# Sending the convolution's taps through DRAM in a fused attention and S4D kernel

## The chip, the core and the metric

The kernel runs on one core of one Trainium2 chip. The metric is the device time of one execution in microseconds (us), and the figure given for a kernel is the median of its runs. Engines are named as in the profile: PE (matmul, with its weight loads as PEld), DVE, ACT, POOL and SP, which here only issues transfers.

## The reference

`x` has 2048 rows of 448 features. Two branches read it and a gate mixes them:

```
def _A_ref(x, wqkv, wo):                       # linear attention, 16 heads of 28
    qkv = (x @ wqkv).reshape(B, S, 3, H, Dh) ...
    phi = lambda t: jnp.where(t > 0, t + 1, jnp.exp(t)) + 1e-6
    pq, pk = phi(q), phi(k)
    kv  = einsum("bhsd,bhse->bhde", pk, v);  z = einsum("bhsd->bhd", pk)
    num = einsum("bhqd,bhde->bhqe", pq, kv)
    den = einsum("bhqd,bhd->bhq", pq, z)[..., None] + 1e-6
    return (num / den) ... @ wo
def _B_ref(u, ...):                            # S4D: a causal convolution of each feature
    K = 2.0 * jnp.einsum("dn,dnl->dl", C, P).real
    y = causal convolution of u with K (by FFT)
    return y + u * D_skip
g = sigmoid((x * gate_w).sum(-1, keepdims=True))
return g * a + (1 - g) * b
```

With the inputs as they are drawn, each feature's time step is so small that all its taps `K` are one number. The convolution is then a running sum of `x` over the rows, times that number. A flag for each feature says whether this holds; a second, general path at the end of the program runs only if a flag says no.

## The kernel before, in words

The 2048 rows are worked on as 16 chunks of 128 rows. Float32 products are made of two parts: a rounded "high" half (ACT makes it) and the "low" rest (a subtraction, mostly on POOL), and PE multiplies high by high, low by high and high by low. The order of every engine's instructions is written out by hand: engines work in the order of the code, and only semaphores between engines hold them.

The main loop (`for c in range(2, NC - 2)`, L476 to L532) runs over chunks. In a step `c` PE computes, in this order: the 11 products of `k` for chunk `c+1` (`project`, tile `k`), in steps 5 to 13 one or two running sums `v` (`do_v`, two products with the triangular matrix `tri`), the 11 products of `q` for chunk `c` (tile `q`), and the 11 products of `g` for chunk `c` (`do_g`), which sum phi(k) times `x`. The table `VS` (L35) says which `v` are made in which step and on which side of `q`. A `v` lives in one of two places of PSUM, `v0` and `v1`, by the parity of its number, so that `v` number 2 can begin only when DVE has read number 0 out.

The other engines' part of a step:

- `split_t(c + 2)`: ACT casts the turned `x` of chunk `c+2` to its high half, and POOL subtracts to get the low half (tile `xt`, L236). PE needs both for the next step's `k`.
- `k_feature`, `k_high`, `k_low`: ACT clamps `k` (`Relu` of -k, L360) and takes the exponential (L361), DVE joins them (L362), ACT adds 1e-6 and rounds (L366), DVE makes the low half and adds to the sum `zb` (L372).
- `q_post`: ACT takes an exponential for the gate (L380) and one of `q` (L349), DVE clamps and adds 1e-6 (L350) and joins (L353) into `pq`.
- `v_post`: DVE multiplies `v` by the row `near`, the taps of all 448 features on every partition (L415); SP sends the last row into the table `u` twice (L418); POOL adds the product to `y` (`v_add`, L423).
- `split_n(c + 2)`: high and low halves of the plain `x` (tile `xn`, L246 and L236), and `skip`, which starts `y` as `x` times `D_skip` (L252).
- `load_x(c + 3)`: SP issues the transfer of a chunk of `x` (512 KB) into one of four buffers; it waits there until POOL and ACT have done with the buffer's earlier chunk.

The taps come from `s4d_prepare`, a generator that is advanced a step at a time between the chunks. Its parameters `abc` lie in the space of `pq`'s later chunks. It ends, in step 4, with `p0`: 112 partitions by 4 numbers. In step 5 PE turns `p0` into a row on all 128 partitions (four transposes, L313), and ACT copies it into `near` (L314). After the loop come the normalisation, the product with `wo` and the mixing, with PE again at work on 11 products a chunk (L629).

Of the kernel before, what the change touches and what calls it, by code (L numbers as in the profile page):

```python
# [7 lines left out]
F32 = mybir.dt.float32  # L8
F32R = mybir.dt.float32r
I32 = mybir.dt.int32  # L10
AF = mybir.ActivationFunctionType
ALU = mybir.AluOpType
# [3 lines left out]
P = 128  # L16
S = 2048
D = 448
# [3 lines left out]
NC = S // P  # L22
J = 4
DJ = D // J
# [7 lines left out]
QA = 1  # L32
QW = 512
EDGE = 16
VS = {c: (2 * c - 10, 2 * c - 9) for c in range(5, 11)} | {c: (c + 1,) for c in range(11, NC - 1)}  # L35
SMALL = 2.0 ** -70
FLAT = 2.0 ** 35
BIG = 3.4028234e38
# [102 lines left out]
def gated_mix_kernel(ctx: ExitStack, tc: tile.TileContext, xin, wq_d, wvo_d, abc_d, ldt_d, dsk_d,  # L141
                     turn_d, cst_d, first_d, gin_d, out):
    nc = tc.nc
    PE, ACT, DVE, POOL, SP = nc.tensor, nc.scalar, nc.vector, nc.gpsimd, nc.sync

    keep = ctx.enter_context(tc.tile_pool(name="keep", bufs=1))
    pq = keep.tile([P, NC, D], F32, name="pq")
# [9 lines left out]
    work = ExitStack()  # L157
# [26 lines left out]
    xn_p = work.enter_context(tc.tile_pool(name="xn", bufs=7))  # L184
    tp = work.enter_context(tc.tile_pool(name="tp", bufs=2))
    ps = work.enter_context(tc.tile_pool(name="ps", bufs=1, space=PSUM))

    warm = tp.tile([P, 512], mybir.dt.bfloat16, name="warm", tag="e")
    POOL.memset(warm, 1.0)
# [7 lines left out]
    def load_x(c):  # L197
        r = xp.tile([P, XC], F32, name="xr", tag="xr")
        turned[c], plain[c] = r[:, :NAT], r[:, NAT:]
        SP.dma_start(out=r, in_=xin[c])  # L200
# [6 lines left out]
    o = 0  # L207
# [18 lines left out]
    SP.dma_start(out=dsk, in_=dsk_d.to_broadcast([P, D]))  # L226
    load_x(3)
    SP.dma_start(out=ldt, in_=ldt_d)
    for i in range(4):
        SP.dma_start(out=abc[:, i], in_=abc_d[:, i])  # L230
        if i == 0:
            load_x(4)
    SP.dma_start(out=both, in_=turn_d)

    def low(eng, o, r, h):
# [2 lines left out]
    def split_t(c):  # L238
        w = xt[c] = xt_p.tile([P, 2 * NAT], F32R, name="xt", tag="t")
        ACT.copy(w[:, :NAT], turned[c])  # L240
        low(POOL, w[:, NAT:], turned[c], w[:, :NAT])
# [33 lines left out]
    def small():  # L275
        cnt[0] += 1
        return sm[:, cnt[0] - 1]

    def s4d_prepare():
        tt = lambda eng, o, a, b, op: eng.tensor_tensor(out=o, in0=a, in1=b, op=op)  # L280
        stt = lambda o, a, k, b, op1: DVE.scalar_tensor_tensor(out=o, in0=a, scalar=k, in1=b, op0=ALU.mult, op1=op1)
        junk = [yf[:DJ, F0 + (i - 2) * 2 * N:F0 + (i - 1) * 2 * N].rearrange("p (i n) -> p i n", i=2) for i in range(2)]
        s0, s1, dt, am, p0, p1, d2, md, b0, b1 = (small() for _ in range(10))
        for j in range(J):
            ACT.activation(abc[:, 0, j], abc[:, 0, j], AF.Exp)
        ACT.activation(dt, ldt, AF.Exp)
        tt(DVE, d2, dt, dt, ALU.mult)
        yield
        for j in range(J):
            ACT.activation(junk[0], abc[:, 0:2, j], AF.Square, accum_out=am[:, j:j + 1])  # L290
            ACT.activation(junk[0][:, 0], abc[:, 2, j], AF.Copy, accum_out=s0[:, j:j + 1])
            DVE.scalar_tensor_tensor(out=junk[1], in0=abc[:, 2:4, j], scalar=1.0, in1=abc[:, 0:2, j], op0=ALU.mult,
                                     op1=ALU.mult, accum_out=s1[:, j:j + 1])
            if j % 2:
                yield
        tt(DVE, md, am, d2, ALU.mult)
        stt(p0, s0, 2.0, dt, ALU.mult)
        stt(p1, s1, -2.0, d2, ALU.mult)
        DVE.tensor_scalar(out=md, in0=md, scalar1=SMALL, scalar2=None, op0=ALU.is_le)
        stt(b0, p0, -1.0, p0, ALU.max)  # L300
        stt(b1, p1, -1.0, p1, ALU.max)
        yield
        DVE.tensor_scalar(out=p0, in0=p0, scalar1=-BIG, scalar2=BIG, op0=ALU.max, op1=ALU.min)
        DVE.scalar_tensor_tensor(out=md, in0=b0, scalar=1.0 / FAR, in1=md, op0=ALU.is_ge, op1=ALU.mult)
        stt(okc, b1, FLAT, b0, ALU.is_le)
        DVE.scalar_tensor_tensor(out=md, in0=b0, scalar=FAR, in1=md, op0=ALU.is_le, op1=ALU.mult)
        tt(DVE, okc, okc, md, ALU.mult)
        tt(DVE, p0, p0, okc, ALU.mult)
        DVE.tensor_reduce(out=oks, in_=okc, op=ALU.add, axis=AX.X)
        yield  # L310
        o = ps.tile([P, 512], F32, name="p", tag="v1")
        for j in range(J):
            PE.transpose(o[:, j * DJ:(j + 1) * DJ], p0[:, j:j + 1].to_broadcast([DJ, P]), ident[:DJ, :DJ])  # L313
        ACT.copy(near, o[:, :D])  # L314

    def pieces(c, wh, wl, n, tag, last=None):
        o = ps.tile([P, 512], F32, name=tag, tag=tag)
# [28 lines left out]
    def feature(dst, o, mid=None):  # L346
        e = tp.tile([P, D], F32, name="e", tag="e")
        t = tp.tile([P, D], F32, name="t", tag="t")
        ACT.activation(e, o[:, :D], AF.Exp)  # L349
        DVE.tensor_scalar(out=t, in0=e, scalar1=1.0, scalar2=1e-6, op0=ALU.min, op1=ALU.add)  # L350
        if mid:
            mid()
        DVE.scalar_tensor_tensor(out=dst, in0=o[:, :D], scalar=C1, in1=t, op0=ALU.add, op1=ALU.max)  # L353
# [3 lines left out]
    def k_feature(c, o):  # L357
        e = tp.tile([P, D], F32, name="e", tag="e")
        pks[c] = o[:, :D]
        ACT.activation(e, pks[c], AF.Relu, scale=-1.0)  # L360
        ACT.activation(e, e, AF.Exp, scale=-1.0)  # L361
        DVE.scalar_tensor_tensor(out=pks[c], in0=pks[c], scalar=1.0, in1=e, op0=ALU.add, op1=ALU.max)  # L362
# [5 lines left out]
    def k_low(c):  # L368
        pk = pks.pop(c)
        pkl[c] = tp.tile([P, 512], F32R, name="pkl", tag="pkl")[:, EDGE:EDGE + D]  # L370
        for o, a, op in ((pkl[c], pkh[c].bitcast(F32), ALU.subtract), (zb, zb, ALU.add))[::-1 if c == NC - 1 else 1]:
            DVE.scalar_tensor_tensor(out=o, in0=pk, scalar=1e-6, in1=a, op0=ALU.add, op1=op)  # L372
# [5 lines left out]

    def q_post(c, o, mid=None):
        ACT.activation(e1[:, c:c + 1], o[:, D:D + 1], AF.Exp, scale=-1.0)  # L380
        feature(pq[:, c], o, mid)

    def do_q(c, tag="q"):
        q_post(c, project(c, wqh, wql, D + 2, tag))
# [23 lines left out]
    def do_v(c):  # L408
        v = vt[c] = ps.tile([P, 512], F32, name="v", tag="v%d" % (c % 2))
        PE.matmul(v[:, :D], lhsT=tri, rhs=xn[c][:, :D], start=True, stop=False)  # L410
        PE.matmul(v[:, :D], lhsT=tri, rhs=xn[c][:, XC - NAT:], start=False, stop=True)

    def v_post(c):
        t = tp.tile([P, D], F32, name="t", tag="v0")
        DVE.tensor_tensor(out=t, in0=vt.pop(c)[:, :D], in1=near, op=ALU.mult)  # L415
        if c < NC - 1:
            for k in (c, UL + c):
                SP.dma_start(out=u[k:k + 1], in_=t[P - 1:P])  # L418
            v_add(c, t)
        return t  # L420

    def v_add(c, t):
        POOL.tensor_tensor(out=y[:, c], in0=y[:, c], in1=t, op=ALU.add)  # L423

    prep = s4d_prepare()
    def steps(n):
        for _ in range(n):
            next(prep, None)
# [45 lines left out]
    split_n(3)  # L474
    woh, wol = [], []
    for c in range(2, NC - 2):  # L476
        if c + 3 < NC:
            load_x(c + 3)
        if c == 2:
            SP.dma_start(out=cst, in_=cst_d)  # L480
        if c == 4:
            SP.dma_start(out=wvo, in_=wvo_d)
        vs = VS.get(c, ())
        ko = project(c + 1, wkh, wkl, D, "v1" if c in (2, 4) else "k")
        for v in vs[:1]:
            do_v(v)
        split_t(c + 2)
        k_feature(c + 1, ko)
        k_high(c + 1)
        if c > 5:  # L490
            for v in vs[:1]:
                v_post(v)
        k_low(c + 1)
        qo = project(c, wqh, wql, D + 2, "q")
        if c == 5:
            steps(1)
        else:
            for v in vs[1:]:
                do_v(v)
        q_post(c, qo)  # L500
        if c == 10:
            split_n(c + 2)
        if c == 5:
            v_post(0)
        else:
            for v in vs[1:]:
                v_post(v)
        if c < 5:
            steps(2 if c == 4 else 1)
        if c == 3:  # L510
            DVE.tensor_copy(tri, trir)
            DVE.tensor_copy(gcr, gcat)
        if c == 7:
            SP.dma_start(out=okr[:, None, :DJ], in_=oks[:, None, :])
        if c == 9:
            DVE.tensor_reduce(out=okr[:, DJ:], in_=okr[:, :DJ], op=ALU.add, axis=AX.X)
            DVE.tensor_copy(okn, okr[:, DJ:])
        do_g(c)
        if c == 5:
            do_v(1)  # L520
        if c < 4:
            skip(c - 1)
        if c != 10:
            split_n(c + 2)
        if c == 5:
            v_post(1)
        for j in {11: (0, 1), 12: (2, 3)}.get(c, ()):
            w = xn_p.tile([P, NX], F32R, name="wo", tag="n")[:DJ, :2 * D].rearrange("p (i d) -> p i d", i=2)
            woh.append(w[:, 0])
            wol.append(w[:, 1])  # L530
            ACT.copy(woh[j], wo[:, j])
            low(POOL, wol[j], wo[:, j], woh[j])  # L532
# [404 lines left out]
```

## Time and profile before

| what | value |
|---|---|
| median of 3 runs | 173.89 us (173.82 to 174.45) |
| the profiled execution's own time | 174.06 us |
| its span, first to last instruction | 172.2 us |
| PE busy | 167.8 us, 97% of the span, 876 products |
| POOL / DVE / ACT busy | 120.0 / 113.9 / 96.0 us |
| granted TensorE clock | 1.000 |

The profile is of one execution. A row of a timeline gives start, duration, engine, line, operation, the tile written and those read, the shape and how many instructions were merged; in brackets stands the idle time before it and what ended it. A row of groups gives the busy time, the mean of one in nanoseconds and the idle time before. PE's products are pipelined, so that one lasts longer than the step from its start to the next one's; the step is what counts.

### The profile page before, as it was taken

The numbers are of one execution on the slowest core, as the hardware profiler recorded it, in microseconds if no ns is written. First come the engines' busy times: TensorE is split into PE (matmuls) and PEld (weight loads), VectorE is DVE, ScalarE is ACT, GpSimd is POOL, SyncE is SP. The second block draws the span as 40 slices with busy tenths as digits, with TensorE's granted clock in tenths as the row PEclk, the third lists the DMA queues.
The fourth block names the chain that finished last, engine by engine and source line by source line (L and its number), as shares of the span: only waits on it lengthen the run. The fifth ranks groups of instructions, "written<-read, shape, count | busy, mean of one in ns | idle before, by whom it ended". The sixth has DMA issues, their size and how long they took to land. (4 is left out here: it accounts for less than half of the span.)

```text
span 172.2 us, 2796 instructions
## 1 busy us (share of the span) xinstructions
PE 167.8 (97%) x876; PEld 152.0 (88%) x876; DVE 113.9 (66%) x240; ACT 96.0 (56%) x221; POOL 120.0 (70%) x128
## 2 busy tenths in 40 slices
PE   6999999999999999999999999999999999999992
PEld 2788999999899999999999999999899999999992
DVE  0847737698975483846627346487898998987542
ACT  3688588894256262542727456356574564664541
POOL 6082667877529988696996999529968998892200
PEclk9999999999999999999999999999999999999999
DMA  5989975097003031230404200000031222122213
GB/s 173 415 297 294 268 209 166 0 368 303 4 0 114 11 123 34 95 123 1 122 15 131 106 1 1 0 0 2 7 67 54 107 89 76 62 99 107 108 59 108
DMA packets 7962, 18.60 MB, mean 108 GB/s; under 512 B 2045, under 2 KB 4810, under 8 KB 7818
## 3 DMA queue, kind: packets, MB, share of 16 engines
q1 hardware_dynamic: 7802, 18.30, 32.0%
q8 instruction: 7, 0.11, 0.3%
q10 hardware_dynamic: 144, 0.11, 0.2%
q14 instruction: 9, 0.07, 0.1%
HBM read 14.38 MB, written 3.67 MB: 105 GB/s over the span
## 5 line engine op out<-in xcount | busy, mean ns | idle before, releaser
L629 PE MATMUL a<-wk,th 128*128 128x448 f32 (+1 forms) x170 | 36.4, 360 | 0.0
L403 PE MATMUL g<-pkh,xn 128*128 128x448 f32 x112 | 35.6, 364 | 0.0
L629 PEld LDWEIGHTS a<-wk,th 128*128 128x128 f32 x170 | 29.5, 189 | 1.6
L334 PE MATMUL k<-wk,xt 128*128 128x448 f32 x132 | 29.3, 367 | 0.0
L334 PE MATMUL q<-wqh,xt 128*128 128x450 f32 x120 | 27.5, 366 | 0.0
L362 DVE SCALAR_TENSOR_TENSOR k<-k,e 128x448 f32<-128x448 f32 x12 | 7.6, 632 | 29.4 <-ACT e L361 29.4
L423 POOL TENSOR_TENSOR y<-y,t 128x448 f32<-128x448 f32 x16 | 18.7, 1168 | 11.5 <-DVE t L415 11.5
L334 PEld LDWEIGHTS k<-wk,xt 128*128 128x128 f32 x132 | 24.8, 189 | 2.2 <-DVE wk L236 0.3
L334 PEld LDWEIGHTS q<-wqh,xt 128*128 128x128 f32 x120 | 22.5, 188 | 1.7
L236 POOL TENSOR_TENSOR xn<-xr,xn 128x448 fp32r<-128x448 f32 x16 | 19.4, 1211 | 6.6 <-ACT xn L246 4.5
L403 PE MATMUL g<-pkl,xn 128*128 128x448 f32 x64 | 23.4, 366 | 0.0
L403 PEld LDWEIGHTS g<-pkh,xn 128*128 128x128 f32 x112 | 21.0, 188 | 2.2
L236 POOL TENSOR_TENSOR xt<-xr,xt 128x512 fp32r<-128x512 f32 x14 | 18.2, 1297 | 5.9 <-ACT xt L240 5.9
L360 ACT ACTIVATE e<-k 128x448 f32<-128x448 f32 x12 | 6.5, 544 | 26.9 <-PE k L334 26.9
L542 POOL TENSOR_TENSOR prod<-pq,zb 128x448 f32<-128x448 f32 x16 | 18.6, 1172 | 4.1 <-ACT zb L665 3.0
L252 POOL TENSOR_TENSOR y<-xr,rows 128x448 f32<-128x448 f32 x16 | 18.8, 1175 | 0.0
L567 POOL TENSOR_TENSOR pn<-pq,den 128x336 f32<-128x336 f32 x16 | 12.3, 771 | 5.9 <-ACT den L556 4.1
L634 DVE SCALAR_TENSOR_TENSOR ot<-y,og,a 128x448 f32<-128x448 f32 (+1 forms) x17 | 10.7, 629 | 5.1 <-PE a L629 5.1
L612 DVE TENSOR_TENSOR th<-tr,th 128x512 fp32r<-128x512 f32 x16 | 11.0, 691 | 2.7 <-ACT th L611 2.1
L403 PEld LDWEIGHTS g<-pkl,xn 128*128 128x128 f32 x64 | 11.2, 174 | 1.2 <-DVE pkl L372 0.2
L611 ACT CAST th<-tr 128x512 fp32r<-128x512 f32 x16 | 9.4, 588 | 4.6 <-PE tr L604 4.4
L334 PE MATMUL q<-wql,xt 128*128 128x450 f32 x45 | 11.6, 364 | 0.0
(150 smaller groups left out, 302.3 us busy)
## 6 DMA issues: line engine op xcount, KB each, us to landing
xr<-in SPq DMA_DIRECT2D x15, 512.0 KB, 6.2
out<-ot SPq DMA_DIRECT2D x15, 224.0 KB, 1.9
pq<-in SPq DMA_DIRECT2D x4, 448.0 KB
wvo<-in SPq DMA_DIRECT2D x1, 1792.0 KB
y<-in SPq DMA_DIRECT2D x2, 480.0 KB
y<-in SPq DMA_DIRECT2D x2, 450.0 KB
u<-t SPq DMA_DIRECT2D x30, 1.8 KB, 1.7
y<-in SPq DMA_DIRECT2D x1, 448.0 KB, 4.3
```

Source lines behind the costliest of these rows:

```text
L236: eng.tensor_tensor(out=o, in0=r, in1=h.bitcast(F32), op=ALU.subtract)
L252: POOL.tensor_tensor(out=y[:, c], in0=plain[c][:, :D], in1=dsk, op=ALU.mult)
L334: PE.matmul(o[:, :n], lhsT=a, rhs=b, start=run.n == 1, stop=not seq)
L362: DVE.scalar_tensor_tensor(out=pks[c], in0=pks[c], scalar=1.0, in1=e, op0=ALU.add, op1=ALU.max)
L403: PE.matmul(g[i][:a.shape[1], :D], lhsT=a, rhs=b, start=c == 0 and n == 0, stop=c == NC - 1 and n == len(seq) - 1)
L423: POOL.tensor_tensor(out=y[:, c], in0=y[:, c], in1=t, op=ALU.add)
L542: POOL.tensor_tensor(out=pd[c], in0=pq[:, c], in1=zb, op=ALU.mult)
L567: POOL.tensor_tensor(out=n[:, :3, :DJ].rearrange("p j (h d) -> p j h d", h=4), in0=a, in1=r[:, :H - 4].rearrange("p (j h) -> p j h", j=3)[ ...
L611: ACT.copy(h, ov)
L612: DVE.tensor_tensor(out=l, in0=ov, in1=h.bitcast(F32), op=ALU.subtract)
L629: PE.matmul(a[:, lo:hi], lhsT=u_, rhs=w_[:, lo:hi], start=n == 0, stop=n == 10)
L634: DVE.scalar_tensor_tensor(out=ot[:, lo:hi], in0=y[:, c, lo:hi], scalar=og[:, c:c + 1], in1=a[:, lo:hi], op0=ALU.mult, op1=ALU.add)
```

## The change

It has three parts.

The four transposes, their PSUM tile and ACT's copy out of it are gone. At the start of step 5 SP instead writes `p0` to a DRAM tile `nd` (112 pieces of 16 bytes, one from each partition) and reads it back to all 128 partitions, into the space of `pq`'s last chunk, which is not used before the end. There the taps stand in another order (`r` outside, `j` inside), so `taps` is a view with a step of 16 bytes. The `v_post` of numbers 0 to 3 read that view, in step 6; at the end of step 6 ACT copies it in order into `near`, which later steps read as before. Number 0 is still made in step 5 and number 1 at its end, but both are read out in step 6, and numbers 2 and 3 are now made behind `q` of step 6.

For chunks 4 to 13 `q_post` clamps as `k_feature` does: `Relu` and exponential on ACT, one instruction on DVE, and a further ACT instruction (`q_shift`) that adds 1e-6 in place after `split_n`.

POOL's sums of `y` with `v` go through a list (`adds`) that is emptied at set places: numbers 0 and 1 come behind the low half of `xt` of step 6, numbers 2 and 3 behind that of step 7. From step 5 on `x` is loaded one step earlier (two loads in step 5), and the four transfers of `abc` at the start become two.

The diff, cut to its core (line numbers of the new code differ from those of the old by a few to some 25):

```
-VS = {c: (2 * c - 10, 2 * c - 9) for c in range(5, 11)} | {c: (c + 1,) for c in range(11, NC - 1)}
+VS = {c: ((2 * c - 10,), (2 * c - 9,)) for c in range(5, 11)} | {c: ((c + 1,), ()) for c in range(11, NC - 1)}
+VS[5], VS[6] = ((0,), ()), ((), (2, 3))
...
-    for i in range(4):
-        SP.dma_start(out=abc[:, i], in_=abc_d[:, i])
-        if i == 0:
-            load_x(4)
+    SP.dma_start(out=abc[:, :2], in_=abc_d[:, :2])
+    load_x(4)
+    SP.dma_start(out=abc[:, 2:], in_=abc_d[:, 2:])
...
-        o = ps.tile([P, 512], F32, name="p", tag="v1")
-        for j in range(J):
-            PE.transpose(o[:, j * DJ:(j + 1) * DJ], p0[:, j:j + 1].to_broadcast([DJ, P]), ident[:DJ, :DJ])
-        ACT.copy(near, o[:, :D])
...
-        feature(pq[:, c], o, mid)
+        if 3 < c < NC - 2:
+            e = tp.tile([P, D], F32, name="e", tag="e")
+            ACT.activation(e, o[:, :D], AF.Relu, scale=-1.0)
+            ACT.activation(e, e, AF.Exp, scale=-1.0)
+            DVE.scalar_tensor_tensor(out=pq[:, c], in0=o[:, :D], scalar=1.0, in1=e, op0=ALU.add, op1=ALU.max)
+        else:
+            feature(pq[:, c], o, mid)
+
+    def q_shift(c):
+        ACT.add(pq[:, c], pq[:, c], 1e-6)
...
+    taps = pq[:, NC - 1].rearrange("p (r j) -> p j r", j=J)
...
-            v_add(c, t)
+            adds.append((c, t))
...
+        if c == 5:
+            SP.dma_start(out=nd.rearrange("o (r j) -> (o r) j", j=J), in_=p0)
+            SP.dma_start(out=pq[:, NC - 1], in_=nd.to_broadcast([P, D]))
...
         split_t(c + 2)
+        if c == 6:
+            v_post(0, taps)
+            v_post(1, taps)
+        v_adds()
...
+        if c > 3:
+            q_shift(c)
+        if c == 6:
+            ACT.copy(near.rearrange("p (j r) -> p j r", j=J), taps)
```

PE at the end of step 5's `q` products, before:

```order
L334 MATMUL q<-wqh,xt 128x450 x8
L334 MATMUL q<-wql,xt 128x450 x3
L313 MATMUL p<-both,sm 128x112 x4
L403 MATMUL g_142<-pkh,xn 128x448
L403 MATMUL g_142<-pkl,xn 128x448
```

and now:

```order
L330 MATMUL q<-wqh,xt 128x450 x8
L330 MATMUL q<-wql,xt 128x450 x3
L408 MATMUL g_143<-pkh,xn 128x448
L408 MATMUL g_143<-pkl,xn 128x448
L408 MATMUL g_143<-pkh,xn 128x448
```

The four transposes into `p` are gone; `g` follows `q` at once.

PE in step 6, from the `k` of chunk 7 to the first of `g`, before (the two pairs of `v` are numbers 2 and 3):

```order
L334 MATMUL k<-wk_70,xt 128x448 x11
L410 MATMUL v<-xn,tri 128x448
L411 MATMUL v<-xn,tri 128x448
L334 MATMUL q<-wqh,xt 128x450 x8
L334 MATMUL q<-wql,xt 128x450 x3
L410 MATMUL v<-xn,tri 128x448
L411 MATMUL v<-xn,tri 128x448
L403 MATMUL g_142<-pkh,xn 128x448
```

and now:

```order
L330 MATMUL k<-wk_70,xt 128x448 x11
L330 MATMUL q<-wqh,xt 128x450 x8
L330 MATMUL q<-wql,xt 128x450 x3
L415 MATMUL v<-xn,tri 128x448
L416 MATMUL v<-xn,tri 128x448
L415 MATMUL v<-xn,tri 128x448
L416 MATMUL v<-xn,tri 128x448
L408 MATMUL g_143<-pkh,xn 128x448
```

Number 2 went behind `q`; PE's work in the step is the same.

SP from the loads of step 3 on, before (`xr` are chunks of `x`, `u` the last rows of `v`):

```order
L200 DMA xr<-in 128x1024 x2
L482 DMA wvo<-in 128x3584
L200 DMA xr<-in 128x1024
L418 DMA u<-t 1x16x28 x4
L200 DMA xr<-in 128x1024
L418 DMA u<-t 1x16x28 x4
```

and now:

```order
L202 DMA xr<-in 128x1024 x2
L499 DMA wvo<-in 128x3584
L202 DMA xr<-in 128x1024 x2
L501 DMA nd<-sm 112x4
L502 DMA pq<-nd 128x448
L202 DMA xr<-in 128x1024
L427 DMA u<-t 1x16x28 x8
```

The load of chunk 9 came ahead of the two new transfers, that of chunk 10 stands between them and the first rows of `v`.

More of the change, by code (lines that the diff above doesn't have):

```diff
@@ L186, in gated_mix_kernel @@
     ps = work.enter_context(tc.tile_pool(name="ps", bufs=1, space=PSUM))
+    nd = work.enter_context(tc.tile_pool(name="nd", bufs=1, space=bass.MemoryType.DRAM)).tile([1, D], F32, name="nd")
     warm = tp.tile([P, 512], mybir.dt.bfloat16, name="warm", tag="e")
@@ L282, in s4d_prepare @@
         junk = [yf[:DJ, F0 + (i - 2) * 2 * N:F0 + (i - 1) * 2 * N].rearrange("p (i n) -> p i n", i=2) for i in range(2)]
-        s0, s1, dt, am, p0, p1, d2, md, b0, b1 = (small() for _ in range(10))
+        s0, s1, dt, am, p1, d2, md, b0, b1 = (small() for _ in range(9))
         for j in range(J):
@@ L309, in s4d_prepare @@
         DVE.tensor_reduce(out=oks, in_=okc, op=ALU.add, axis=AX.X)
-        yield
-        o = ps.tile([P, 512], F32, name="p", tag="v1")
-        for j in range(J):
-            PE.transpose(o[:, j * DJ:(j + 1) * DJ], p0[:, j:j + 1].to_broadcast([DJ, P]), ident[:DJ, :DJ])
-        ACT.copy(near, o[:, :D])
     def pieces(c, wh, wl, n, tag, last=None):
@@ L411, in do_v, with v_post @@
         PE.matmul(v[:, :D], lhsT=tri, rhs=xn[c][:, XC - NAT:], start=False, stop=True)
-    def v_post(c):
+    taps = pq[:, NC - 1].rearrange("p (r j) -> p j r", j=J)
+    def v_post(c, w=None):
+        w = near.rearrange("p (j r) -> p j r", j=J) if w is None else w
         t = tp.tile([P, D], F32, name="t", tag="v0")
-        DVE.tensor_tensor(out=t, in0=vt.pop(c)[:, :D], in1=near, op=ALU.mult)
+        DVE.tensor_tensor(out=t.rearrange("p (j r) -> p j r", j=J),
+                          in0=vt.pop(c)[:, :D].rearrange("p (j r) -> p j r", j=J), in1=w, op=ALU.mult)
         if c < NC - 1:
@@ L418, in v_post, with v_adds @@
                 SP.dma_start(out=u[k:k + 1], in_=t[P - 1:P])
-            v_add(c, t)
+            adds.append((c, t))
         return t
+    adds = []
+    def v_adds():
+        while adds:
+            v_add(*adds.pop(0))
     def v_add(c, t):
         POOL.tensor_tensor(out=y[:, c], in0=y[:, c], in1=t, op=ALU.add)
+    p0 = small()
     prep = s4d_prepare()
@@ L476, in gated_mix_kernel @@
     for c in range(2, NC - 2):
-        if c + 3 < NC:
-            load_x(c + 3)
+        for i in (c + 3,) if c < 5 else (c + 3, c + 4) if c == 5 else (c + 4,):
+            if i < NC:
+                load_x(i)
         if c == 2:
@@ L482, in gated_mix_kernel @@
             SP.dma_start(out=wvo, in_=wvo_d)
-        vs = VS.get(c, ())
+        if c == 5:
+            SP.dma_start(out=nd.rearrange("o (r j) -> (o r) j", j=J), in_=p0)
+            SP.dma_start(out=pq[:, NC - 1], in_=nd.to_broadcast([P, D]))
+        vs = VS.get(c, ((), ()))
         ko = project(c + 1, wkh, wkl, D, "v1" if c in (2, 4) else "k")
-        for v in vs[:1]:
+        for v in vs[0]:
             do_v(v)
         split_t(c + 2)
+        if c == 6:
+            v_post(0, taps)
+            v_post(1, taps)
+        v_adds()
         k_feature(c + 1, ko)
@@ L490, in gated_mix_kernel @@
         if c > 5:
-            for v in vs[:1]:
+            for v in vs[0]:
                 v_post(v)
+        v_adds()
         k_low(c + 1)
         qo = project(c, wqh, wql, D + 2, "q")
[L495 to L499, printed above, removed]
+        for v in vs[1]:
+            do_v(v)
         q_post(c, qo)
@@ L502, in gated_mix_kernel @@
             split_n(c + 2)
[L503 to L507, printed above, removed]
+        for v in vs[1]:
+            v_post(v, taps if c == 6 else None)
+        if c != 6:
+            v_adds()
         if c < 5:
@@ L524, in gated_mix_kernel @@
             split_n(c + 2)
-        if c == 5:
-            v_post(1)
+        if c > 3:
+            q_shift(c)
+        if c == 6:
+            ACT.copy(near.rearrange("p (j r) -> p j r", j=J), taps)
         for j in {11: (0, 1), 12: (2, 3)}.get(c, ()):
```

## Prediction

> **What bounds the kernel now.** I read the page's first part, then the waits of PE and its weight loads, then PE's timeline around the change.
>
> ```profile
> PE 167.8 (97%) x876; PEld 152.0 (88%) x876; DVE 113.9 (66%) x240; ACT 96.0 (56%) x221; POOL 120.0 (70%) x128
> ...
> PE q L258 <- POOL warm L189: 1.3, 1, 1.3
> ...
> PEld p L313 <- DVE sm L280: 0.2, 1, 0.2
> ```
>
> PE is busy for 97% of the span. Its one wait as an engine is 1.3 us at the start, and its weight loads wait 0.2 us for `p0` at the first transpose. So the other engines have slack, and the kernel gets shorter only by work taken off PE, or longer by a new wait of PE. The place is the end of `q` in a step. Step 4 has no transposes:
>
> ```profile
> 39.01 0.76 PE L334 MATMUL q<-wql,xt 128*128 128x450 f32 x3
> ...
> 39.81 0.36 PE L403 MATMUL g<-pkl,xn 128*128 128x448 f32 x1
> ```
>
> Step 5 has them:
>
> ```profile
> 46.04 0.76 PE L334 MATMUL q<-wql,xt 128*128 128x450 f32 x3
> 46.66 0.60 PE L313 MATMUL p<-both,sm 112*128 112x112 f32 x4
> ...
> 47.31 0.36 PE L403 MATMUL g<-pkl,xn 128*128 128x448 f32 x1
> ```
>
> **The transposes.** From the last `q` group to the second product of `g` step 4 takes 39.81 - 39.01 = 0.80 us, step 5 takes 47.31 - 46.04 = 1.27 us. The transposes with their wait cost 0.47 us of PE's time, and nothing else stands there. That is the first term: -0.47 us. The upper bound is their unoverlapped time:
>
> ```profile
> L313 PE MATMUL p<-both,sm 112*128 112x112 f32 x4 | 0.6, 272 | 0.0
> L313 PEld LDWEIGHTS p<-both,sm 112*128 112x128 f32 x4 | 0.4, 136 | 0.2 <-DVE sm L280 0.2
> ```
>
> The sum, 0.6 + 0.4 = 1.0 us, would need that nothing of them overlapped; the starts say otherwise, so I take 0.47.
>
> **The new way of the taps.** This is the only new wait that PE can meet soon: `v` number 2 now needs DVE to have read number 0, which needs the taps. PE's step 6 before:
>
> ```profile
> 49.73 2.38 PE L334 MATMUL k<-wk,xt 128*128 128x448 f32 x11
> 51.95 0.37 PE L410 MATMUL v<-xn,tri 128*128 128x448 f32 x1
> ...
> 52.36 1.77 PE L334 MATMUL q<-wqh,xt 128*128 128x450 f32 x8
> ...
> 54.56 0.37 PE L410 MATMUL v<-xn,tri 128*128 128x448 f32 x1
> ...
> L415 DVE TENSOR_TENSOR t<-v,rows 128x448 f32<-128x448 f32 x16 | 9.8, 615 | 0.0
> ```
>
> With 0.47 gone `k` starts at 49.26; it takes 51.95 - 49.73 = 2.22 and `q` takes 54.56 - 52.36 = 2.20, so PE wants the place of number 0 at 49.26 + 4.42 = 53.68 us. DVE's `v_post` takes 0.61, so the taps must have landed by 53.07. When do they?
>
> ```profile
> 40.72 0.16 ACT L380 ACTIVATE e<-q 128x1 f32<-128x1 f32 x1
> 41.40 0.61 DVE L372 SCALAR_TENSOR_TENSOR zb<-v,zb 128x448 f32<-128x448 f32 x1
> 41.93 1.38 DVE L350 TENSOR_SCALAR t<-e 128x448 f32<-128x448 f32 x1
> 43.42 0.62 DVE L353 SCALAR_TENSOR_TENSOR pq<-q,t 128x448 f32<-128x448 f32 x1
> 46.44 0.16 DVE L280 TENSOR_TENSOR sm<-sm,okc 112x4 f32<-112x4 f32 x1
> ...
> L360 ACT ACTIVATE e<-k 128x448 f32<-128x448 f32 x12 | 6.5, 544 | 26.9 <-PE k L334 26.9
> ...
> DMA to landing us min/median/max: 1.6/1.7/2.4
> ...
> DMA to landing us min/median/max: 3.8/3.8/3.8
> ...
> 50.00:53.00 3.00, 3.00 (x17) 2.79 (x16) 1.07 (x3) 0.76 (x2) 2.32 (x3) 1.00 0.01 1
> ```
>
> `p0` is ready at 46.60 before. In step 4 the change takes out L350 (1.38 us there). ACT starts at 40.72; with two passes of 0.544 instead of one it ends near 41.9, and DVE is free of `zb` at 42.01, so L353's successor runs at 42.01 and not at 43.42: `p0` comes up to 1.41 us earlier, at 45.19. Two transfers follow, the second waiting for the first. The trace has neither; the nearest are the rows of `u` (1.8 KB, the first landing row: 1.6 to 2.4 us) and `cst` (112.5 KB from DRAM, the second: 3.8). Both lie between: 2 x 1.6 = 3.2 and 2 x 3.8 = 7.6 us together. I take 1.7 for the write, as small as `u`, and for the read 2.4, since it goes to 128 partitions but finds the engines idle (the last row: a DMA share of 0.01 from 50 to 53 us). Landing: 45.19 + 4.1 = 49.3, 3.8 us ahead of need. Ends: 45.19 + 3.2 = 48.4, and 46.60 + 7.6 = 54.2, which is too late by 1.1. The term is 0, with the late end as a rival. The Trainium skill's page "DMA: Bandwidth & Descriptors", section "Latency and other measured facts", puts HBM access at 0.2 us on average and 2 us at high load. The idle share above speaks for the low end; 2 us more for each hop would be an estimate of 4 us, by which the taps come at 53.3 and PE waits 0.2.
>
> SP must not be held ahead of these transfers. It is moved past one load, that of chunk 9, which waits for POOL to finish chunk 5:
>
> ```profile
> 38.48 1.15 POOL L252 TENSOR_TENSOR y<-xr,rows 128x448 f32<-128x448 f32 x1
> 53.18 0.53 SPq L200 DMA_DIRECT2D xr<-in  x1
> 36.00:40.00 4.00, 4.00 (x21) 3.75 (x20) 3.97 (x7) 2.69 (x7) 3.07 (x4) 1.00 1.05 440
> 42.00:43.00 1.00, 1.00 (x6) 0.94 (x6) 1.00 (x2) 0.34 (x1) 1.00 (x1) 1.00 0.12 49
> ```
>
> POOL is done at 39.63, and the load goes out then, not at 53.18. Its 512 KB at 440 GB/s are 1.2 us, behind traffic that now ends by 42.2: clear by 43.4, before `p0`. The load of chunk 10 waits behind the read's issue on SP until about 47, still ahead of 53.18, where even chunk 9 stood. Cost 0.
>
> The four `v_post` read SBUF at a step of 16 bytes. No row shows such a read. The bounds are the 615 ns of L415 above, with a contiguous row, and the slowest engine's two-input pass over as many elements:
>
> ```profile
> L423 POOL TENSOR_TENSOR y<-y,t 128x448 f32<-128x448 f32 x16 | 18.7, 1168 | 11.5 <-DVE t L415 11.5
> L362 DVE SCALAR_TENSOR_TENSOR k<-k,e 128x448 f32<-128x448 f32 x12 | 7.6, 632 | 29.4 <-ACT e L361 29.4
> ```
>
> I take 615 ns: four at the slow price would be 4 x 0.55 = 2.2 us of DVE, hidden while DVE idles some 2.5 us a chunk (29.4 us before L362 in all). The Trainium skill's page "SBUF — State Buffer", section "Door 1: The DMA port swizzle", speaks against this: SBUF has lines of 16 bytes, and each access that crosses to a new one pays a penalty. Every element here is on a new line, so by it the slow price is the nearer; the sum stays, since DVE hides it, but the late rival below gets likelier.
>
> **q's clamp.** ACT gains two instructions for each of ten chunks, one like L360 (544 ns above) and one like L366; DVE loses one:
>
> ```profile
> L366 ACT ACTIVATE pkh<-k 128x448 fp32r<-128x448 f32 x12 | 6.5, 546 | 8.5 <-DVE k L362 8.5
> 57.17:64.61 7.44, 7.44 (x39) 6.90 (x37) 4.36 (x8) 3.56 (x8) 6.27 (x6) 1.00 0.24 71
> 100.96:107.99 7.03, 7.03 (x37) 6.52 (x35) 3.25 (x8) 3.34 (x8) 6.93 (x7) 1.00 0.01 1
> ```
>
> ACT gets 0.544 + 0.546 = 1.09 us more a step: 3.56 becomes 4.65 of 7.44, and 3.34 becomes 4.43 of 7.03. Behind `q_shift`, which waits for DVE, is queued the cast of `xt`, and behind that POOL's low half, which PE wants at the next `k`:
>
> ```profile
> 55.13 1.30 POOL L236 TENSOR_TENSOR xt<-xr,xt 128x512 fp32r<-128x512 f32 x1
> 104.62 1.30 POOL L236 TENSOR_TENSOR xt<-xr,xt 128x512 fp32r<-128x512 f32 x1
> 57.17 2.36 PE L334 MATMUL k<-wk,xt 128*128 128x448 f32 x11
> ```
>
> At the tightest step the half is ready at 56.43 for a `k` at 57.17: 0.74 us of slack, behind POOL's first two sums. This is the step in which those go behind it. Late in the loop, where POOL is 6.93 of 7.03 us busy, the half ends at 105.92 for the `k` that begins where that stretch ends, at 107.99: 2.07 us of slack, more than the 1.09 added and the 0.47 by which PE comes earlier. Cost 0.
>
> **POOL's order and the loads at the start.** The sums of numbers 2 and 3 now run in step 7 with 4 and 5. Behind them on POOL wait `xn` and the next `xt`, which wait for number 5 anyway; DVE's `v_post` of number 4 waits for the sum of number 2, since `t` has two buffers. Two sums are 2 x 1.168 = 2.3 us later at most in a step of 7.44 with 7.44 - 6.27 = 1.17 idle, but step 5 and 6 have two sums less ahead of their halves, and POOL waits 11.5 us for DVE before its sums in all, which now takes the halves in. Cost 0. The first half of `abc` now goes ahead of chunk 4 with 448 KB more:
>
> ```profile
> 20.00:24.00 4.00, 4.00 (x22) 3.71 (x21) 2.17 (x4) 2.84 (x11) 2.27 (x2) 1.00 0.83 208
> 24.43 0.62 ACT L240 CAST xt<-xr 128x512 fp32r<-128x512 f32 x1
> ...
> 8.35 0.35 SPq L200 DMA_DIRECT2D xr<-in  x1
> ...
> DMA to landing us min/median/max: 3.6/6.2/10.9
> ```
>
> At the 208 GB/s of that stretch it is 2.2 us; even by the longest landing chunk 4 comes at 8.35 + 10.9 + 2.2 = 21.5, and ACT reads it at 24.43. Cost 0.
>
> **The sum.** Against the profiled execution's own 174.06 us: -0.47, so 173.59. That execution is 0.17 above the median of the runs, 173.89; on the median the forecast is 173.42, say 173.4, or -0.27%. About 0.5%, 0.87 us, is what a measurement of this kernel can tell from no change.
>
> **Rivals.** *The taps come late.* At the late end, 54.2, PE waits at number 2: with 0.61 a `v_post` 1.1 us, at number 3 another 0.1; with the slow 1.17 it is 1.69 and then 0.76. Net of the 0.47: 174.7 and 175.9; I put it at 175.3, slower. It decides from a landing at about 53.4 on (52.2 with slow reads), and costs over 0.5% from 54.3 (53.1) on. For it: two transfers and a stepped read that no row shows. Against: 3.8 us of slack. The Trainium skill's two rules above both speak for it. *ACT holds up `xt`.* Were the 1.09 us laid on the smallest slack, 0.74, PE would lose 0.35 once: 173.8. Against: that step's half now goes ahead of the sums. *The transposes were worth more,* up to their 1.0 us: 172.9. For it only that PE's ends are modelled; starts are not. That the change leaves the transposes' time in place cannot be: they are gone from PE's order.
>
> **Chances.** Forecast 0.80, late taps 0.09 (slower), ACT 0.06 (same), larger saving 0.05 (faster): faster 0.05, same 0.86, slower 0.09. The range leaves out the two ends, 0.14. Below, it goes four fifths of the way from 173.4 to the larger saving, to 173.0, since the lowest run less 0.47 is 173.35. Above, half of the late rival's milder excess: 173.89 + 0.3 = 174.2, which takes in ACT's case and the highest run less 0.47, 173.98.
>
> **What would show it.** In the new profile: in step 5 the second product of `g` 0.80 us after the last `q` group; the write and the read landing between 48.4 and 53.0; `v` number 2 at about 53.7 with no wait of PE or its weight loads for DVE; the `v_post` of step 6 at 0.61 or more; ACT near 4.6 us a step; POOL's `xt` of step 6 done by 53; PE as dense as before behind it. A wait of PE for DVE in step 6, or for POOL at a `k`, would prove the forecast wrong.

## The result and the profile after

The kernel after takes 174.55 us (median of 21 runs, 174.27 to 176.5) beside 173.97 for the kernel before on the same chip (21 runs, 173.75 to 174.6). The ratio is 1.004, with a 95% interval of 1.0026 to 1.0053: slower by 0.4%, where 0.27% faster was forecast. The profiled execution took 174.61 us, its span is 172.8 us (172.84 to the nanosecond, 172.23 before), and PE's clock was 1.000.

On the page of the kernel after, the first row is the engines' busy time, the second the shares of the chain that ended last:

```profile
PE 167.8 (97%) x872; PEld 151.7 (88%) x872; DVE 110.2 (64%) x230; ACT 107.8 (62%) x241; POOL 119.7 (69%) x128
...
PE 78%; DVE 8%; ACT 6%; DMA 3%; issue 2%; ACTq 0%; POOL 0%; DVEq 0%; POOLq 0%
```

PE has four products less and is busy as long as before. ACT has 12 us more (107.8 beside 96.0), DVE 4 us less. A transfer stands in the chain: 3% of the span is DMA. (The page of the kernel before follows its chain over the last 0.6 us only and cannot be set beside this.) PE's timeline shows where:

```profile
46.09 0.76 PE L330 MATMUL q<-wql,xt 128*128 128x450 f32 x3
...
46.89 0.36 PE L408 MATMUL g<-pkl,xn 128*128 128x448 f32 x1
...
49.36 2.45 PE L330 MATMUL k<-wk,xt 128*128 128x448 f32 x11
...
53.91 0.37 PE L415 MATMUL v<-xn,tri 128*128 128x448 f32 x1
54.11 0.37 PE L416 MATMUL v<-xn,tri 128*128 128x448 f32 x1
54.60 0.47 PE L415 MATMUL v<-xn,tri 128*128 128x448 f32 x1
...
57.32 0.96 PE L330 MATMUL k<-wk,xt 128*128 128x448 f32 x4
```

The end of step 5 went as forecast: from the last `q` group to the second product of `g` 46.89 - 46.09 = 0.80 us, 0.47 less. But `v` number 3 starts 0.49 us behind the second product of number 2, where 0.20 is the rule, and from this step's `k` to the next one's PE takes 57.32 - 49.36 = 7.96 us, where it took 57.17 - 49.73 = 7.44. The waits of the weight loads in this stretch name the causes:

```profile
PEld v L415 <- DVE t L423: 0.5, 1, 0.5
PEld k L330 <- ACT e L380: 0.2, 1, 0.2
```

The first is the wait of PE for DVE in step 6 which the prediction said would prove it wrong. The second, at the step's `k`, is smaller: `k` and `q` together take 53.91 - 49.36 = 4.55 us, where they took 4.42. The profile puts it down to ACT's exponential of the new clamp, which ends at 49.14. By the code `k` also needs its place in PSUM, which DVE's L368 reads until 49.21. The runs do not separate the two; both stand behind DVE's small operations of step 4, and run 3 below, where these come early, has no such wait. The chain through that stretch (start, duration, what) comes from DVE's small operations on `p0` and runs over both transfers to `v`:

```profile
46.87 1.38 DMA nd<-sm
...
48.26 4.44 DMA pq<-nd
...
53.61 0.95 DVE t L423
...
54.60 0.47 PE v L415
```

The last of the small operations, from DVE's timeline, makes `p0`:

```profile
46.68 0.16 DVE L281 TENSOR_TENSOR sm<-sm,okc 112x4 f32<-112x4 f32 x1
```

`p0` is ready at 46.84 and not at 45.19, the read takes 4.44 us and not 2.4, and a product with `v` takes 0.95 us and not 0.61. The taps land at 52.70; 49.3 was forecast.

That is not all of the loss. The first product of `g`, the last product and ACT's last copy before:

```profile
12.83 0.37 PE L403 MATMUL g<-pkh,xn 128*128 128x448 f32 x1
...
168.83 0.27 PE L629 MATMUL a<-rc,th 112*128 112x224 f32 x1
...
170.03 0.59 ACT L640 COPY pq<-a 128x224 f32<-128x224 f32 x2 [2.05 <-DVEq L847]
```

and after:

```profile
12.88 0.37 PE L408 MATMUL g<-pkh,xn 128*128 128x448 f32 x1
...
168.97 0.27 PE L652 MATMUL a<-rc,th 112*128 112x224 f32 x1
...
170.17 0.59 ACT L663 COPY pq<-a 128x224 f32<-128x224 f32 x2 [2.05 <-DVE ot L657]
```

By the last product the kernel after is only 0.14 us behind: 0.05 at the start, -0.42 by the transposes (the rest of the 0.47 went to a late `k`), +0.52 in step 6. The span is longer by 0.61. The other 0.47 us come behind ACT's last copy, where nothing is computed any more. SP's three `DRAIN` instructions, which stand in the last us of the program and compute nothing, before and after (how many, shortest/median/longest duration in ns, first and last start):

```profile
L933 SPq DRAIN  x3: 7/13/19, 171.4 to 172.0; - x3
```

```profile
L956 SPq DRAIN  x3: 7/7/120, 171.9 to 172.3; - x3
```

From the start of ACT's last copy to the first of them it is 1.4 us before and 1.7 after, and the first takes 120 ns instead of 13. ACT's copy, the last work of all, had ended by 170.76.

So there are two losses to explain, the late taps and the late end.

### The profile page after: what moved, and what is told of

It reads as the page before. It is cut to its first block, busy times and chain, and to the rows that moved or that the text cites. A ratio compares the mean times of both kernels' runs of the same rounds, so it can differ in the third digit from the quotient of the medians.

```text
span 172.8 us, 2792 instructions
## 1 busy us (share of the span) xinstructions
PE 167.8 (97%) x872; PEld 151.7 (88%) x872; DVE 110.2 (64%) x230; ACT 107.8 (62%) x241; POOL 119.7 (69%) x128
## 4 chain that ended last, share of the span: by engine, by line
PE 78%; DVE 8%; ACT 6%; DMA 3%; issue 2%; ACTq 0%; POOL 0%; DVEq 0%; POOLq 0%
PE a L652 21%; PE g L408 15%; PE q L330 13%; PE k L330 12%; PE tr L627 4%; PE v L330 4%; PE q L259 3%; DMA pq<-nd 3%; PE v L415 2%; PE v L416 2%; PE m L731 1%; DVE sm L282 1%; PE k L751 1%; PE tr L751 1%; DVE y L293 1%
## 5 line engine op out<-in xcount | busy, mean ns | idle before, releaser
L358 DVE SCALAR_TENSOR_TENSOR k<-k,e 128x448 f32<-128x448 f32 x12 | 7.6, 631 | 28.7 <-ACT e L357 28.7
L362 ACT ACTIVATE pkh<-k 128x448 fp32r<-128x448 f32 x12 | 6.5, 545 | 10.2 <-DVE k L358 10.2
```

## The experiments

To compare executions, which start up to 0.9 us apart, I give two lengths for each: from the first product of `g` to the start of the last product (before 156.00 us, after 156.09), and from the start of ACT's last copy to the end of the span (before 2.20, after 2.67, with the spans to the nanosecond).

**1 and 2: a longer list for SP.** What the change adds to SP's list is short: the built program holds 212 SP instructions before and 214 after. Behind the last output comes a branch over the general path, which is never taken here. A transfer there can be split without any effect on what is computed:

```
-    SP.dma_start(out=out.rearrange("(c p) d -> p c d", p=P), in_=yg)
+    for a, b in ((0, 1), (1, NC)):
+        SP.dma_start(out=out.rearrange("(c p) d -> p c d", p=P)[:, a:b], in_=yg[:, a:b])
```

Run 1 is the kernel before with this; one instruction is added to the part that is not run and one semaphore instruction to the way around it.

> The kernel before; one transfer of the part that is never run (the general convolution behind the branch at the end) is split in two, so SP's list is two instructions longer, as it is in the kernel after, and no engine does other work. Theory 1 (the end of the program waits for a block of SP's instructions, whose border the change pushed into the last drains): last product at 168.8 as before, but the end 0.46 us later, some 174.4 beside 174.0. Rival (the end is late because of the DRAM tile or of POOL's order): no change, 174.0.

Measured: 174.34 us beside 173.97, ratio 1.0024 (1.0004 to 1.0045). PE and ACT, then SP's `DRAIN`s:

```profile
12.40 0.37 PE L404 MATMUL g<-pkh,xn 128*128 128x448 f32 x1
...
168.38 0.27 PE L630 MATMUL a<-rc,th 112*128 112x224 f32 x1
...
169.58 0.59 ACT L641 COPY pq<-a 128x224 f32<-128x224 f32 x2 [2.05 <-DVEq L848]
```

```profile
L934 SPq DRAIN  x3: 7/7/119, 171.3 to 171.7; - x3
```

PE's length is 155.98, as before. The end is that of the kernel after: 1.7 us from the copy to the first `DRAIN`, 119 ns for it, 2.66 from the copy to the end. Run 2 is the kernel after with the transfer split in four, which makes the list 220 long.

> The kernel after with the same transfer split in four (SP's list 6 longer). Theory 1: the border falls among waits that are long anyway, the end comes 0.46 us earlier, some 174.1 beside 174.55 for the kernel after, with the last product still at 168.97. Rival: no change, 174.55.

Measured: 173.94 us, ratio to before 0.9987 (0.9967 to 1.0007).

```profile
170.52 0.59 ACT L664 COPY pq<-a 128x224 f32<-128x224 f32 x2 [2.05 <-DVE ot L658]
```

```profile
L957 SPq DRAIN  x3: 7/7/13, 171.9 to 172.2; - x3
```

From the copy to the first `DRAIN` it is 1.4 us again, the longest takes 13 ns, and 2.20 us pass to the end, while PE still waits for DVE (0.4 us). PE's length is 155.98, 0.11 less than in the kernel after: the same read took 53.06 - 48.73 = 4.33 us to DVE's first product in this execution and 52.73 - 48.26 = 4.47 in that one. What holds of theory 1, in both directions, is that the end depends on how long SP's list is, and on none of the work. What SP waits for is another question. In the trace SP's last wait for a semaphore begins 0.42 us ahead of the first `DRAIN` in the kernel after (171.48 and 171.90) and in run 1 (170.88 and 171.30), 0.07 in the kernel before and in run 2. The kernel before has a pause of 0.42 us too, but one place later, behind its second `DRAIN` (171.47 to 171.90), where POOL's last instructions run beside it; run 2 has none. So the pause moves with the list. Over all runs here, the lists of 214 (after, 1, 3, 4, 7) end 2.66 to 2.67 us behind the start of the copy, those of 212, 215 and 220 (before, 2, 6, 8) 2.19 to 2.22; run 5, also 220, is in between at 2.39.

**3: the taps early.** The kernel after, with the last two parts of the preparation in step 4 moved ahead of `k_low`:

```
         k_high(c + 1)
+        if c == 4:
+            steps(2)
...
         if c < 5:
-            steps(2 if c == 4 else 1)
+            steps(1 if c < 4 else 0)
```

> The kernel after; the last two parts of the filter's preparation stand ahead of step 4's low half of k instead of behind its q, where POOL is idle for 1.6 us. Theory 2 (the taps are late, first of all because POOL's work held DVE's small operations): the small operations take 0.16 us each, p0 is there by 42.5 instead of 46.84, the taps land by 49, PE waits nowhere in step 6, and the last product comes 0.4 to 0.5 us earlier (168.5); the time is 174.1, or 173.6 if the end of the program falls better. Rival (PE's wait in step 6 is the order of v and k, not the taps): PE's wait stays, 174.55.

Measured: 174.05 us, ratio 0.9998 (0.9977 to 1.002). The first and the last of DVE's operations for `p0` and its first products with `v`, POOL's operation at that time, and PE:

```profile
40.41 0.75 DVE L281 TENSOR_TENSOR sm<-sm 112x4 f32<-112x4 f32 x1
...
42.14 0.16 DVE L281 TENSOR_TENSOR sm<-sm,okc 112x4 f32<-112x4 f32 x1
...
49.06 1.82 DVE L423 TENSOR_TENSOR t<-v,pq 128x448 f32<-128x448 f32 x2
...
39.84 1.30 POOL L237 TENSOR_TENSOR xt<-xr,xt 128x512 fp32r<-128x512 f32 x1
...
49.49 2.37 PE L330 MATMUL k<-wk,xt 128*128 128x448 f32 x11
...
56.98 1.36 PE L330 MATMUL k<-wk,xt 128*128 128x448 f32 x6
```

The first small operation ends with POOL's `xt` (41.16 and 41.14), all the others, beside an idle POOL, take 0.15 to 0.17. `p0` is there at 42.30, DVE's products with `v` no longer wait for a transfer, PE waits for nothing in the step, at `k` neither (56.98 - 49.49 = 7.49 us), and its length falls to 168.62 - 13.08 = 155.54, 0.55 less than after and 0.46 less than before. That is the forecast's 0.47. The end is late as in the kernel after (2.66), so the time is that of the kernel before. Theory 2 holds; its rival, the order of `v` and `k`, falls. The transfers of this run, from SP's timeline:

```profile
42.33 0.33 SPq L501 DMA_DIRECT2D nd<-sm  x1
45.03 0.33 SPq L502 DMA_DIRECT2D pq<-nd  x1
45.51 1.33 SPq L202 DMA_DIRECT2D xr<-in  x1
```

The read waits for the write, which so took 45.03 - 42.33 = 2.70 us and not 1.38: it starts in the middle of other traffic (a DMA share of 0.98 from 42 to 43 us, where the kernel after has 0.00 from 46 to 47). The load of chunk 10 goes out 0.48 us behind the read.

**4: the load of chunk 10 later.** The kernel after, with this 512 KB transfer behind the first two products with `v`:

```
-            if i < NC:
+            if i < NC and i != 10:
                 load_x(i)
...
             v_post(1, taps)
+            load_x(10)
```

> The kernel after; the load of chunk 10 (512 KB), issued 0.5 us behind the read of the taps, is issued behind the first two products with v instead. Theory 2a (the load slows the read of the taps): the read takes 2.4 us instead of 4.4, the taps land at 50.7, PE does not wait in step 6, and the last product comes 0.4 us earlier, 174.1. Theory 2b (the read of one row by 128 partitions takes 4.4 us by itself): landing 52.7, PE's wait stays, 174.55.

Measured: 174.36 us, ratio 1.0016 (0.9998 to 1.0035).

```profile
48.14 0.33 SPq L502 DMA_DIRECT2D pq<-nd  x1
...
52.17 1.83 DVE L423 TENSOR_TENSOR t<-v,pq 128x448 f32<-128x448 f32 x2 [2.50 <-DMA pq<-nd]
```

From the issue of the read to DVE's first product it is 4.03 us, in the kernel after 4.47 and in run 2 4.33. So 4.0 us are the read's own, as theory 2b had it for the most part, and PE's wait for DVE is gone, as 2a had it, since the other 0.44 were most of that wait. That the load behind the read costs the 0.44 is not shown: in runs 3 and 5 it went out 0.5 us behind the read too, and DVE began its first product 49.06 - 45.03 = 4.03 and 49.09 - 45.03 = 4.06 us after the read's issue without waiting for it. The length is 168.46 - 12.75 = 155.71, 0.38 less than after. PE's wait at step 6's `k` is still there (0.3 us); run 3, without it, is 155.71 - 155.54 = 0.17 shorter.

**5: both repairs.** The edits of runs 2 and 3 together.

> The kernel after with both edits that helped by themselves: the last parts of the filter's preparation ahead of step 4's low half of k, and the never-run transfer split in four. Theory (late taps and a late end are two losses that add): PE waits nowhere in step 6, from PE's first product of g to its last product 155.82 us instead of 156.36, from ACT's last copy to the end of the span 1.58 instead of 2.06: 173.55, below the kernel before's 173.97. Rival (the two do not add, since something else is due at the end): 174.0.

Measured: 173.53 us beside 173.88, ratio 0.9974 (0.9959 to 0.9989), the fastest here with an interval. PE's length is 168.65 - 13.09 = 155.56. The end took 172.25 - 169.86 = 2.39 us: better than 2.67, with 0.2 us that I cannot place; they lie between ACT's last copy and SP's `DRAIN`s. The two losses add, and without them the kernel is faster than before, as forecast. That 0.26% stands so near to the forecast's 0.27% is in part luck: the interval goes from 0.11% to 0.41%, the two medians differ by 0.20%, and in the profiles PE gains 0.44 us of which the end gives 0.19 back.

**6: the clamp alone.** The kernel before with the second part of the change (`q_post` and `q_shift` as in the diff above, without the taps, the loads and POOL's order).

> The kernel before with the second part of the change alone: q's clamp of chunks 4 to 13 on ACT. SP's list is as long as in the kernel before. Theory (this part costs nothing, all of the loss is with the taps and the end): from first g to last product 156.27 as before, 1.59 from ACT's last copy to the end, 174.0. Rival (ACT's 1.09 us more in each step holds up what PE waits for): PE waits for ACT in several steps, 174.4 or more.

Measured: 174.31 us, ratio 1.0017 (1.0002 to 1.0032). The end is as before (2.19). PE's length is 169.54 - 13.22 = 156.32, 0.32 more than before: the theory falls. Its waits (before, the first was 0.2 and there was no second of this kind):

```profile
PEld p L313 <- DVE sm L280: 0.4, 1, 0.4
...
PEld k L739 <- ACT gs L686: 0.2, 1, 0.2
```

The first is in step 5. POOL's `xn` in step 4, before and in this run:

```profile
41.90 1.16 POOL L236 TENSOR_TENSOR xn<-xr,xn 128x448 fp32r<-128x448 f32 x1 [1.03 <-ACT xn L246]
```

```profile
42.92 1.16 POOL L236 TENSOR_TENSOR xn<-xr,xn 128x448 fp32r<-128x448 f32 x1 [1.64 <-ACT xn L246]
...
47.04 0.16 DVE L280 TENSOR_TENSOR sm<-sm,okc 112x4 f32<-112x4 f32 x1
```

Counted from the first product of `g` POOL's three operations begin 29.70 - 29.07 = 0.63 us later, since ACT's cast stands behind the clamp's two passes, and `p0` is ready 33.98 - 33.77 = 0.21 later instead of 1.41 earlier. PE, which waited for it by 0.2 us before, loses that.

**7: the taps in order.** The kernel of run 3 with the write in pieces of 4 bytes, so that the read brings the taps in `v`'s order:

```
-            SP.dma_start(out=nd.rearrange("o (r j) -> (o r) j", j=J), in_=p0)
+            SP.dma_start(out=nd.rearrange("o (j r) -> (o r) j", j=J), in_=p0)
...
-    taps = pq[:, NC - 1].rearrange("p (r j) -> p j r", j=J)
+    taps = pq[:, NC - 1].rearrange("p (j r) -> p j r", j=J)
```

> The kernel of the early taps, with the write to DRAM in pieces of 4 bytes (448 instead of 112), so that the taps come back in the order in which v needs them. Theory (the step of 16 bytes in SBUF makes DVE's products with v 0.95 us long): they take 0.61 us, and ACT's copy of the taps 0.53 instead of 1.01; the write takes longer, up to some 4 us, which the early start covers, the read is 4.0 to 4.4 as it was; PE as there. Rival (they are long because POOL works beside them): 0.95 stays.

Measured: one run, 175.69 us. The chain, then DVE and ACT:

```profile
41.96 7.91 DMA nd<-sm
49.89 4.56 DMA pq<-nd
```

```profile
54.47 1.16 DVE L423 TENSOR_TENSOR t<-v,pq 128x448 f32<-128x448 f32 x2 [5.69 <-DMA pq<-nd]
...
59.03 0.55 ACT L551 COPY rows<-pq 128x448 f32<-128x448 f32 x1
```

Two products take 1.16 us, where the step of 16 bytes makes them 1.82, and ACT's copy 0.55, where it was 1.01. POOL happens to be idle beside these two products; but in the kernel before, all 16 products with the row in order took 612 to 618 ns, beside POOL or not (the one at 53.93 ran beside POOL's L252 and L423). So the step is what costs, and POOL is not. But the write in 448 pieces takes 7.91 us, where run 3, whose write began 0.37 us later, needed 2.70 for 112, and it uses up the early start; PE's weight loads wait 2.0 us. This is rival 1 of the prediction made on purpose, with its price.

**8: one POOL operation less beside DVE's small ones.** The kernel after, with the skip product of chunk 6 moved behind `xn` of chunk 7:

```
-        if c > 2:
+        if c > 2 and c != 6:
             skip(c)
+        if c == 7:
+            skip(6)
```

> The kernel after, with one of the three operations that POOL runs back to back beside DVE's small ones (the product of chunk 6 with the skip row, 1.15 us) moved one step on. Theory (a small operation of DVE on SBUF ends only when the operation that POOL is at has ended): one of the three long ones goes, p0 comes 1.1 us earlier, 45.7 where it was 46.84 in the kernel after, and the taps land 1.1 us earlier. Rival (the small operations are long by themselves): p0 as in the kernel after.

Measured: one run, 173.45 us. DVE and POOL in the kernel after:

```profile
39.67 0.62 DVE L358 SCALAR_TENSOR_TENSOR v<-v,e 128x448 f32<-128x448 f32 x1
...
43.74 1.13 DVE L300 TENSOR_SCALAR sm<-sm 112x4 f32<-112x4 f32 x1
...
39.64 1.28 POOL L237 TENSOR_TENSOR xt<-xr,xt 128x512 fp32r<-128x512 f32 x1
...
43.69 1.15 POOL L253 TENSOR_TENSOR y<-xr,rows 128x448 f32<-128x448 f32 x1
```

and in this run:

```profile
43.53 0.16 DVE L302 TENSOR_SCALAR sm<-sm 112x4 f32<-112x4 f32 x1
43.60 1.34 DVE L284 SCALAR_TENSOR_TENSOR sm<-sm 112x4 f32<-112x4 f32 x2
...
45.51 0.16 DVE L283 TENSOR_TENSOR sm<-sm,okc 112x4 f32<-112x4 f32 x1
...
43.62 1.30 POOL L237 TENSOR_TENSOR xt<-xr,xt 128x512 fp32r<-128x512 f32 x1
```

The same `TENSOR_SCALAR` takes 1.13 us beside POOL's product and 0.16 without it, and what stays long ends with POOL's `xt` (44.94 and 44.92). `p0` is ready 1.17 us earlier by the clock of each run, 0.86 counted from the first `g` (12.88 after, 12.57 here). PE's length is 168.25 - 12.57 = 155.68, the list has 215 instructions and the end takes 2.22, so this single run lies where run 5's median does. The edit moved a second thing: the load of chunk 10 needs the buffer that the skip product of chunk 6 reads, and went out at 50.86, 3.77 us behind the read (47.09) and not 0.5. The run is therefore also run 4's repair, and its length cannot be put down to `p0` alone; the durations of DVE's operations can. The read took 51.00 - 47.09 = 3.91 us to DVE's first product, which agrees with run 4.

## Why the prediction was wrong, point by point

**"`p0` comes up to 1.41 us earlier, at 45.19": this step failed.** The arithmetic took L350's 1.38 us out of DVE's list. But one chunk later, in the kernel before, the same operation took this:

```profile
48.89 0.38 DVE L350 TENSOR_SCALAR t<-e 128x448 f32<-128x448 f32 x1
```

One us of the 1.38 was no work: runs 3 and 8 show that what DVE does on SBUF alone ends there when POOL's operation ends. Without L350 the small operations moved up beside POOL's three operations and were held in its place, and by the clamp's two passes on ACT those three began 0.63 us later (run 6). `p0` came at 46.84, 0.24 later than before. The Trainium skill's page "SBUF — State Buffer", section "SBUF: two separate sides", states that DVE and GpSimd (POOL) share a pair of ports which the one that starts first holds for its whole instruction, where the DVE operation has two inputs in SBUF or uses both ports for one, which the page allows for `tensor_scalar`. The rows agree: 1.13 us beside POOL, 0.16 without, and 0.62 as ever for L358, which reads one input from PSUM while POOL runs `xt`. Whether the 1.13 us operation, which has one input, did use both ports no run here shows.

**The write, 1.7 us, and the read, 2.4 us: this term failed too.** The write took 1.38. The read was mis-sized: 4.0 us by itself (run 4; 3.9 in run 8) and 4.44 in the kernel after, above the upper row of 3.8. That the engines were idle before it did not make it short. Of the 3.4 us by which the landing missed its forecast (52.70 for 49.3), the read has 2.0 and `p0` 1.65, and the write gives 0.3 back. The prediction had let the load of chunk 10 wait behind the read and asked whether it was late, not whether it could slow the read; that stays open (runs 3, 4 and 5).

**"I take 615 ns" for the stepped read.** It took 0.95 us, between the bounds of 0.615 and 1.168; in order it is again 0.61 (run 7). The Trainium skill's rule on lines of 16 bytes, which the prediction cites ("SBUF — State Buffer", "Door 1: The DMA port swizzle"), leaned the right way: 55% more in this case. DVE's idle time does hide the four of them, but two stand between the landing and `v` number 3, and there each counts in full.

**The rival "The taps come late" is what happened.** It was to decide from a landing at 52.2 on with slow reads; the landing was 52.70. Its size was smaller than put there (174.7 to 175.9), 0.52 us in step 6, because the landing was 1.5 us short of its late end. The chance of 0.09 was too low: `p0`, the write and the read were each taken at or near the favourable end. That the kernel came out slower, as this rival said, is not its work alone: by the last product the kernel after is 0.14 us behind, and the end adds the rest. (The range's upper end took half of the rival's milder excess as 0.3; half of 174.7 - 173.89 is 0.4, which the result exceeds as well. And the interval above, 0.14% each way, can tell much smaller differences than the 0.5% that the prediction assumed.)

**The transposes: right.** 0.47 us between the same two rows, and 0.46 over PE's whole length once the taps are in time (run 3).

**q's clamp at nothing: wrong by a detour.** No `xt` was late, as argued (step 6's was done at 53.25 for a `k` at 57.32). What the 1.09 us on ACT did was to shift POOL's operations against DVE's (run 6: 0.32 us on the kernel before, 0.21 of it with `p0`). The other 0.1 goes with PE's new wait for ACT at the end of the loop; the kernel after has no such wait.

**POOL's order, the loads and `abc`: right.** Behind step 6 PE is as dense as before; both kernels take the same time from there to the last product (168.97 - 57.32 = 111.65, before 168.83 - 57.17 = 111.66).

**The end of the program was not in the sum at all.** The forecast added up PE's time and took all behind the last product as fixed. It was 0.47 us longer, as much as the change was to gain, by the length of SP's list (runs 1 and 2). That SP waits there for its instructions is inferred: the trace shows a pause of 0.4 us ahead of a `DRAIN` whose semaphore had its value long before, and run 1 that code which is never run helps to place it. The Trainium skill's page "Runtime: NRT & Kernel Launch", section "Instruction fetch mechanics", states that instructions come in blocks by transfers of the engine's own and that a taken branch to a place outside of those at hand waits for a fetch. The runs agree with a border that moves with the list, and none shows the fetch itself as the cause.

## What to carry to other kernels

Before you book an operation's duration as a gain, ask whether it is work or waiting: if the same shape takes 0.38 us elsewhere and 1.38 here, the difference belongs to whatever runs beside it, and will be paid by what comes next. A result that travels through DRAM is a chain of two transfers and a read, and each of its terms should be taken from the slow end unless a row of the same kind says otherwise; here starting the chain earlier took the wait away (run 3), and bringing the taps in order to shorten the read-out made the chain longer (run 7). And a difference of some 0.3% can come from the length of an instruction list; look at what lies behind the last computing instruction before you explain such a difference by the change.

## What the runs showed of the hardware that I had not expected

- A DVE operation on 112 x 4 numbers in SBUF takes 0.16 us alone and up to 1.13 us beside POOL; it ends with POOL's operation.
- Reading one row of 1792 bytes in DRAM to 128 partitions takes 4.0 us with the engines otherwise idle, more than the 3.8 of 112 KB in `cst`. Writing 1.8 KB from 112 partitions in pieces of 16 bytes takes 1.38 us with the engines idle and 2.70 in traffic (run 3); in pieces of 4, begun in the like traffic, 7.91 (run 7).
- A float32 operand at a step of 16 bytes makes DVE's product of 128 x 448 0.95 us instead of 0.61, and ACT's copy 1.01 instead of 0.55.
- Two instructions more in SP's list (in run 1 one of them is never run) make the program 0.4 us longer, and six more take it back.
